# Local attention: blocks of 58 queries on two strips of 64 rows become blocks of 26 queries on four strips of 32, and VectorE turns the probabilities

## The chip, the core and the metric

One core of a Trainium2 chip runs one launch of the program. Its engines work side by side and wait for each other by semaphores: TensorE (PE in the profile, its weight loads PEld), VectorE (DVE), ScalarE (ACT), GpSimd (POOL), and SyncE (SP), which issues most transfers. Matmuls write to PSUM (eight banks here, tiles named `ps`); the other tiles lie in SBUF. The metric is the device time of one execution in microseconds.

## The reference, cut to what matters

Attention over 8 batches, 8 heads, 576 positions and a head size of 64 has two branches whose outputs are added. One averages q, k and v over groups of four and attends fully over 144 positions. The other, which the change rewrites, attends locally: a query sees the keys less than four positions away.

```
pos = np.arange(S)
mask = np.abs(pos[:, None] - pos[None, :]) < factor        # factor 4
scores = scale * np.matmul(q, k.transpose(0, 1, 3, 2))
scores = np.where(mask, scores, -1e9)
scores = scores - np.max(scores, axis=-1, keepdims=True)
attn = np.exp(scores)
attn = attn / (np.sum(attn, axis=-1, keepdims=True) + 1e-09)
out_local = np.matmul(attn, v)
```

The sum of the branches is the input x (8 x 576 x 512) of an MLP with a gate over positions: h = gelu(x w_in) is halved into u and v, v is normalized over its features and multiplied by a 576 x 576 matrix along the positions, and x + (u * v_s) w_out is the result.

## The kernel before

The work is cut into 32 attention pairs (a batch and two heads, which share the 128 partitions) and eight MLP passes, one a batch. Every step is a small task with a name: a letter or two and the pair's number (`S12`), or batch and part (`u3.4`). One table, `ORDER`, lists the more than 2,200 tasks in the order in which they are emitted, with a letter for the engine where there is a choice (V, A, P). Each engine runs its instructions in that order; `place` gives the buffers out by the same table. The MLP's matmuls keep fp32 accuracy by splitting both factors in a high and a low part and taking three products (lines 665 and 743).

A pair's tasks, local branch first:

- `S` (`scores`, L420): windows of 64 queries by 64 keys, ten a head, which advance by 58. The head's 64 features are the contraction. A window and a head write 64 rows of PSUM, so the ten windows of a head fill two strips of 64 rows in two banks. For the first four pairs (`EARLY_S`) an identity matmul puts the additive mask in PSUM first (L413).
- `ma`, `mb` (L428): VectorE adds the mask for the later pairs, PSUM to SBUF. `mx` takes the maxima, `nx` scales them to biases, `ea` and `eb` (L482) run ten exponentials on ScalarE, one for each column block, each with its own bias and its row sum. `re`, `rc`, `np` normalize (L504).
- `T` and a part of `U` (L512, L522): TensorE transposes the five 128x128 blocks of probabilities to PSUM; `pa` and `pb` copy them to SBUF.
- `D` (`av`, L573): values by probabilities, 64-row contractions, 20 matmuls on 64x64 parts of the array, and `xa`, `xb` (L580) add the other branch.

The averaged branch has `qs`, `ks`, `vs` (sums of four), `Y` (L442, scores), `my`, `ny`, `ec`, `nq`, its own transposes in `U` and `t` (L517), the copies `pc` and `pe`, `d` (`av_d`, L552: 72-row contractions) and `od`. Then `xh`, `xl`, `xc` split x for the MLP. Every non-transposing fp32 matmul of attention leaves two records in the trace. In the table the attention blocks stand between groups of MLP matmuls, mostly one or a few at a time.

Of the kernel before, what the change touches and what calls it, by code (L numbers as in the profile page):

```python
# [21 lines left out]
QB = 58  # L22
KB = 64
NT = 10
NTP = NT // 2
QPAD = QB * (NT - 1) + KB
HALF = S // 2
NS = 5
LEFT = S - 4 * P
XW = S + LEFT  # L30
# [54 lines left out]
lk0/S lq0/A ks0/V wy7 small wy2 lk1/A wuy7 qs0/V wby7 wqy7 wy0 lq1/S Y0 wy5 wy3 lq2 lk2 my0 wz7 wy1 wy4 wuy2 wz1 lq3  # L85
wz5 wy6 lk3 S0 wz2 lq4 wz0 wfy7 wby2 ny0/A wty7/P ks1/P wz4 wr1 lw3 lk4 wr2 lv0/S ec0 wqy2 wuy0 wby0 wqy0 why7/A
wuy5 mx0 wq2 lw2 lw0/S S1 wz6 lv1/S lk5 wr4 nx0/A qs1/P wfy0 lq5 wr7 wr0 lw1/S wq0 wfy2 wuy3 wby3 wby5 ea0 wqy3 eb0
wqy5 mx1 wuz7 re0/A wuy4 wty0/P wfy3 qs2/P nx1/V ea1 Y1 my1 wfy5 wly7/V ny1/V rc0 wby4 ec1 eb1 wqy4 wuz5 ks2/P
wty3/P wty5/P why5/V why0/V why3/V S2 mx2 np0/P Y2 my2 nx2/V ny2/V T0 re1/V wly5/V wfy4 pa0/V rc1 nq0/P wty2/P U0
pb0/V ec2 t0 wby1 ea2 wuy1 wuy6 wqy1 pc0/A wly3/P wty4/P wby6 nq1/P S3 wbz4 wqy6 np1/P why2/A wfy1 pe0/V qs3/P ks4/P  # L90
t1 mx3 wfy6 ks3/V eb2 wqz4 re2/A T1 wty6/P nx3/A wur2 pa1/A ea3 why4/A rc2 U1 qs4/V pb1/V pc1/A wuz2 d0 od0 lv2 wz3
np2/V why6/V wbz5 pe1/V wfz4 wqz5 T2 wty1/P nq2/P pa2/A wuz4 wly6/P wly4/P wly2/P wly0/P Y3 why1/V D0 wfz5 my3 xa0
U2 pb2/V xb0 pc2/V S4 wuz0 eb3 wur1 ny3/A ma4 xh0/V t2 pe2/A ec3 d1 mb4 wuz1 re3/A wuz6 wbz7 mx4 rc3 wbz6 Y4 od1 my4
D1 wbz0 qs5/P wtz5/P xl0/P np3/P nq3/P xc0 nx4/A wqz7 xa1 ea4 wqz6 ny4/A eb4 wq3 lv3 lw5 lw4 wq1 lk6 d2 wfz7 od2
wfz6 xb1 b lq6 wr3 wly1/V S5 lq7 lv4 ma5 xh1/V mb5 wtz7/P whz7/V mx5 wtz6/P t3 xl1/P ec4 re4/A whz5/A wqz0 rc4 vk2.0
D2 T3 nx5/A vk1.0 nq4/P xa2 pa3/A U3 wfz0 vk2.1 xb2 pb3/V eb5 np4/V vk1.1 xh2/V pc3/A wtz0/P ea5 wlz7/P wbz1 t4
pe3/V U4 vk0.0 wtz4/P xl2/P T4 pa4/A wqz1 pb4/A whq3/A ks6/V ks5/V qs6/V wfz1 d3 pc4/A od3 wur0 pe4/A wbz2 wbz3 wqz2
whz0/A wqz3 wuz3 vk1.2 D3 vs4 wr6 wr5 xa3 xb3 xh3/A wtz1/P whz1/A vk0.1 wlz0/P Y5 wfz2 d4 my5 od4 xl3/P wbr1 ny5/A
wur3 wqr1 wq4 lk7 wfz3 wur4 ec5 wlz1/V wur7 re5/A whz6/A wbr3 wqr3 wfr1 qs7/V wbr5 xc2 xc1 wtz3/P wlz5/P xc3 wtz2/P
wtr1/P rc5 np5/P wlz6/P vk2.2 vk0.2 v0.2 v0.1 v0.0 D4 wfr3 vg0.0 whz2/A whr1/A vg0.2 wqr5 whz3/A xa4 ks7/V vb0.0 xb4  # L100
v0.3 vg0.3 vp0.0 S6 vb0.2 ma6 wfr5 vn0.0 lk8 Y7 vg0.1 whq4/A wur5 whq1/A whz4/A vb0.1 wlz2/V mb6 my7 wlz3/P v0.4
u0.6 u0.4 u0.5 va0.4/A wbr7 vj0.4 xh4/A whq0/A whq2/A lq8 vp0.2 vp0.1 wtr5/P wtr3/P vg0.4 ny7/A u0.7 whr5/A wur6
whr3/A nq5/V vb0.3 vn0.1 wlz4/V vn0.2 wlq1/V wlq4/P vp0.3 u0.0 wlq2/P ua0.6 vh0.1/A ua0.4 ua0.5 u0.1 u0.2 vh0.0/A
ua0.7 vh0.2/A vb0.4 wqr7 ua0.0 vn0.3 vh0.3/A wbr2 wlr5/V wlq0/V wlr3/P vp0.4 vn0.4 wlq3/V vl0.0/V vl0.3/V vl0.2/V
wqr2 xl4/V vl0.1/P vh0.4/A u0.3 ua0.1 ua0.2 ua0.3 vl0.4/P wfr7 wfr2 Y6 mx6 my6 T5 s0.0 wlr1/P xc4 wtr7/P ks8/P qs8/P
sa0.0 wtr2/P sm0.0/P lv5 s0.1 U5 s0.2 ec7 wbr0 s0.3 pa5/A nx6/A whr7/A ea6 wbr4 sa0.1 wbr6 pb5/A wqr0 eb6 wqr6 wfr0
# [12 lines left out]
ea10 vh1.4/V vl1.4/V eb10 S11 os0.1 ma11 mb11 xb9 vl1.3/P vs10 lk13 lw11 os0.0 u1.5 lq13 re10/V rc10 s1.0 s1.4 mx11
ua1.6 ua1.5 np10/P T10 nq10/P U10 nx11/V ua1.7 xh9/A sa1.0 my11 eb11 ks13/P s1.2 ny11/V pa10/V pb10/V pc10/V t10  # L120
pe10/V sm1.0/P ks12/P xl9/P ea11 ec11 re11/A s1.1 sa1.2 sm1.2/V rc11 d10 sa1.1 s1.3 od10 lv11 np11/V sa1.4 sm1.4/V
sm1.1/V sa1.3 T11 nq11/P xc9 s1.5 U11 s1.6 t11 gh1.0/V sm1.3/V vs11 pa11/A s1.7 gh1.1/A pb11/A gl1.0/V sa1.5 sm1.5/V
pc11/A sa1.6 pe11/A gh1.2/A gl1.1/P D10 d11 od11 sm1.6/V sa1.7 sm1.7/V xa10 xb10 gl1.2/P S12 gh1.3/A D11 qs13/P lq14
ma12 Y12 gl1.3/V S13 xa11 mb12 ma13 mb13 my12 xb11 lk14 o1.7 Y13 xh11/A mx13 my13 nx13/V eb13 xh10/A o1.3 o1.0 o1.4
lk15 lq15 lw12 mx12 oa1.0 xl11/P xl10/P ks14/P xc10 lw13 o1.6 lv12 oa1.4 ny12/V xc11 vs12 nx12/A ny13/V ec13 ea12
ec12 qs15/V eb12 o1.1 v2.0 re12/A rc12 np12/P v2.1 ea13 oa1.1 nq12/P re13/V rc13 ks15/P qs14/V v2.2 T12 o1.5 vg2.1
t12 vg2.2 vg2.0 os1.0 oa1.6 vb2.1 oa1.7 np13/V os1.3 oa1.5 os1.2 u2.6 U12 pa12/V pb12/V vp2.1 vb2.2 vp2.2 vb2.0
vn2.1 o1.2 T13 u2.2 ua2.6 vp2.0 pc12/V vn2.0 pe12/V vh2.0/A vn2.2 nq13/V oa1.2 v2.4 va2.4/A vj2.4 vg2.4 vb2.4 pa13/V
ua2.2 u2.0 d12 od12 v2.3 ua2.0 D12 vp2.4 vl2.0/P lv13 vh2.2/V oa1.3 vn2.4 xa12 xb12 vg2.3 vh2.4/V vh2.1/A vs13 Y15
Y14 S14 U13 ma14 mb14 mx14 lq16 os1.1 u2.1 vl2.4/P vb2.3 pb13/A pc13/A xh12/V nx14/A t13 u2.3 u2.5 pe13/V ua2.1 my14  # L130
# [64 lines left out]
oa7.5 os7.2 oa7.7 os7.3.1  # L195
"""
EARLY_S, EARLY_D = 4, 4
SIZES = {"ps": 8, "X": 10, "R": 40}
WIDTH = {"ps": 512, "X": XW, "R": QPAD}


# [758 lines left out]
```

## Time and profile before

| | |
|---|---|
| time, median of 2 runs | 603.26 us (602.92 to 603.61) |
| the profiled execution's own time | 602.69 us |
| its span, first to last instruction | 600.9 us |
| busy: TensorE, VectorE, ScalarE, GpSimd | 578.5, 435.2, 336.2, 324.2 us |
| granted TensorE clock | 1.00 |
| moved by DMA | 58.08 MB |

The span is what the trace covers; 1.8 us of the execution lie around it. Matmuls overlap, so the length of one (0.2 to 0.4 us) is not what it costs; the distance between starts is. Rows of the timeline merge equal neighbours: start, time from the first start to the last end, line, shape, count.

### The profile page before, as it was taken

What the parts mean: (1) busy time and instruction counts of PE and PEld (TensorE: products, weight loads), DVE (VectorE), ACT (ScalarE), POOL (GpSimd) and SP (SyncE); (2) the same over time, 40 slices, a digit from 0 to 9 for tenths busy, and PEclk for the clock granted to TensorE, in tenths of its full rate; (3) what the DMA queues carried; (4) which work ended last, traced back from release to release, by engine and by line L of the source; (5) the groups of instructions that cost most, each with busy time, mean ns of one, the idle gap of its engine ahead of it and who ended that gap; (6) DMA issues with size and microseconds to landing.
All of it is one profiled execution on the core that took longest, in us unless ns stands there. A gap on an engine that the chain in (4) does not pass through costs nothing.

```text
span 600.9 us, 16628 instructions
## 1 busy us (share of the span) xinstructions
PE 578.5 (96%) x6544; PEld 524.9 (87%) x6544; DVE 435.2 (72%) x925; ACT 336.2 (56%) x1270; POOL 324.2 (54%) x417
## 2 busy tenths in 40 slices
PE   5599999999999999999999999999999999999997
PEld 3477889988999989988999889998999888998997
DVE  5999999758784798938786469774779478744652
ACT  5998875754936367264484537547473657811210
POOL 3788788644854255533365456534668554441221
DMA  8994103643040341404304123303225310201102
GB/s 311 349 313 147 42 21 97 192 122 100 25 124 23 100 144 44 124 0 140 106 25 140 62 83 113 112 22 102 61 83 168 96 28 1 80 5 39 40 1 79
DMA packets 28493, 58.08 MB, mean 97 GB/s; under 512 B 3328, under 2 KB 3584, under 8 KB 28416
## 3 DMA queue, kind: packets, MB, share of 16 engines
q1 hardware_dynamic: 28128, 56.43, 29.6%
q8 instruction: 51, 0.84, 0.6%
q10 hardware_dynamic: 288, 0.60, 0.3%
q14 instruction: 26, 0.21, 0.1%
HBM read 47.58 MB, written 9.44 MB: 95 GB/s over the span
## 4 chain that ended last, share of the span: by engine, by line
PE 79%; DVE 10%; DMA 4%; ACT 4%; issue 1%; POOL 1%; SPq 0%; DVEq 0%; ACTq 0%; POOLq 0%
PE ps L743 49%; PE ps L665 15%; PE ps L552 3%; PE ps L573 3%; PE ps L517 3%; PE ps L420 2%; DMA R<-in_w_in_dram 2%; PE ps L512 2%; PE ps L442 2%; ACT X L482 1%; DMA R<-in_qT_dram 1%; DVE R L222 1%; DMA X<-in_vw_dram 1%; DVE R L787 1%; DVE st L695 1%
## 5 line engine op out<-in xcount | busy, mean ns | idle before, releaser
L743 PE MATMUL ps<-wsg_h,R 128*128 128x288 f32 x576 | 122.8, 300 | 0.7 <-POOL R L734 0.7
L743 PE MATMUL ps<-R,wout_h 128*128 128x288 f32 x512 | 111.2, 302 | 0.4 <-DVE X L428 0.3
L482 ACT ACTIVATE X<-X,nb 128x64 f32<-128x64 f32 x280 | 93.5, 338 | 13.0 <-DVE nb L461 12.6
L743 PEld LDWEIGHTS ps<-wsg_h,R 128*128 128x128 f32 x576 | 93.7, 189 | 1.7 <-POOL R L734 0.9
L743 PE MATMUL ps<-wsg_l,R 128*128 128x288 f32 x320 | 92.6, 295 | 0.0
L743 PEld LDWEIGHTS ps<-R,wout_h 128*128 128x128 f32 x512 | 84.1, 188 | 3.6 <-issue 1.2
L743 PE MATMUL ps<-X,win_h 128*128 128x288 f32 x256 | 78.5, 307 | 1.0 <-DVE R L580 1.0
L743 PE MATMUL ps<-X,win_l 128*128 128x288 f32 x256 | 75.6, 295 | 0.0
L743 PE MATMUL ps<-R,win_h 128*128 128x288 f32 x256 | 75.6, 295 | 0.0
L743 PE MATMUL ps<-R,wout_l 128*128 128x288 f32 x256 | 75.6, 295 | 0.0
L706 POOL TENSOR_TENSOR rs<-rs,nhalf 128x1 f32<-128x1 f32 (+1 forms) x40 | 24.2, 606 | 85.9 <-DVE rs L697 85.8
L665 PE MATMUL ps<-win_h,X 128*128 128x512 f32 x160 | 65.4, 409 | 0.0
L665 PE MATMUL ps<-win_l,X 128*128 128x512 f32 x160 | 63.0, 394 | 0.0
L743 PEld LDWEIGHTS ps<-wsg_l,R 128*128 128x128 f32 x320 | 60.2, 188 | 0.0
L222 ACT COPY R<-ps 72x288 f32<-72x288 f32 (+2 forms) x87 | 32.7, 408 | 42.3 <-PE ps L517 14.9
L482 ACT ACTIVATION_READ_ACCUMULATOR X<-X,nb 128x1 f32 x280 | 53.4, 191 | 0.0
L743 PEld LDWEIGHTS ps<-X,win_h 128*128 128x128 f32 x256 | 48.2, 188 | 3.6 <-issue 1.6
L665 PE MATMUL ps<-win_h,R 128*128 128x512 f32 x128 | 50.5, 395 | 0.0
L222 ACT CAST R<-R 128x576 fp32r<-128x576 f32 (+2 forms) x35 | 22.6, 646 | 49.0 <-DVE R L714 21.0
L780 DVE SCALAR_TENSOR_TENSOR vs<-ps,small_sb,b_sb 128x288 f32<-128x288 f32 x64 | 32.3, 508 | 23.4 <-PE ps L743 21.7
L743 PEld LDWEIGHTS ps<-R,win_h 128*128 128x128 f32 x256 | 48.3, 189 | 0.3
L743 PEld LDWEIGHTS ps<-R,wout_l 128*128 128x128 f32 x256 | 48.2, 188 | 0.0
(102 smaller groups left out, 1417.1 us busy)
## 6 DMA issues: line engine op xcount, KB each, us to landing
X<-in_vw_dram SPq DMA_DIRECT2D x32, 320.0 KB
R<-in_v_dram SPq DMA_DIRECT2D x64, 144.0 KB
R<-in_kT_dram SPq DMA_DIRECT2D x31, 293.0 KB
R<-in_qT_dram SPq DMA_DIRECT2D x31, 293.0 KB
out_dram<-R SPq DMA_DIRECT2D x31, 288.0 KB
R<-in_w_in_dram SPq DMA_DIRECT2D x16, 256.0 KB
R<-in_w_out_dram SPq DMA_DIRECT2D x8, 256.0 KB
R<-in_w_sgT_dram SPq DMA_DIRECT2D x5, 288.0 KB
```

The lines of the kernel that those rows point to most:

```text
L222: (nc.scalar.copy if e == "A" else ENG[e].tensor_copy)(**kw)
L420: nc.tensor.matmul(out=sp[i][os, c * KB:(c + 1) * KB], lhsT=q[hs, t * QB:t * QB + KB], rhs=k[hs, t * QB:t * QB + KB], start=not early, sto ...
L442: nc.tensor.matmul(out=st["sdv"][n][os], lhsT=qd2[par][hs, i * 48:i * 48 + HD], rhs=st["kd"][hs], start=True, stop=True)
L482: nc.scalar.activation(out=st["ms"][:, t, :], in_=src, func=AF.Exp, bias=st["nb"][:, i * NTP + c:i * NTP + c + 1], scale=scale, accum_out= ...
L512: nc.tensor.transpose(out=t1[:, c * P:(c + 1) * P], in_=st["ms"][:, 2 * c:2 * c + 2, :], identity=ident_sb)
L517: nc.tensor.matmul(out=out[:, i * P:(i + 1) * P], lhsT=st["pd"][:, n, keys], rhs=ident2[:, i % 2], is_transpose=True, start=True, stop=True)
L552: nc.tensor.matmul(out=dn[hs].rearrange("p (i m) -> p i m", i=3), lhsT=st["v4"][kt][:, f, hs] if early_d else st["vd"][:, kt, hs], rhs=pdt ...
L573: nc.tensor.matmul(out=at["ps", "o", g, i][hs, c * QB:(c + 1) * QB], lhsT=v[ks, c, hs], rhs=pt[ks, c, h ^ i], start=True, stop=True)
L665: nc.tensor.matmul(out=acc, lhsT=r32(l), rhs=r32(w[:, k, DM:DF]), start=(i == 0 and ks[0] == 0), stop=(i == len(ops) - 1 and ks[-1] == KT ...
L706: nc.gpsimd.tensor_tensor(out=rs[0:n], in0=rs[0:n], in1=nhalf[0:n], op=ALU.pow)
L743: nc.tensor.matmul(out=acc[:, 0:HALF], lhsT=r32(l), rhs=r32(r), start=(first and n == 0), stop=(last and n == len(ops) - 1))
L780: nc.vector.scalar_tensor_tensor(out=vsb[i], in0=at["ps", "m", b, "s", i][:, 0:HALF], scalar=g_sb[:, i // 2:i // 2 + 1], in1=b_sb[:, half( ...
```

## The change

Local attention is cut into windows of 26 queries and 32 keys. The 23 windows of a head (24 places) lie on four strips of 32 rows, six column blocks each, so scores of a head fill one bank of 128 x 192. Rows of a window now hold one head only in each bank, and a block is 32 x 32, which VectorE can turn within SBUF. Part by part:

- `S`: 48 matmuls with a contraction of 64 and an output of 32 rows by 32 columns, with `tile_position` naming the part of the array; the mask matmuls have 192 columns instead of 320.
- Softmax: masked (`ma`, `mb`), maximum (`mx`), then the maximum is subtracted as an operation of its own (`sb`, on VectorE or GpSimd; for the first four pairs `ma` and `mb` do it straight from PSUM). One exponential covers all 384 columns, and the row sums are a VectorE reduce (`rw`). `nx`, `eb` and the accumulating forms are gone.
- `tr`: one VectorE transpose by 32x32 blocks takes the place of `T`, of the first matmul of `U`, and of `pa` and `pb`. `U` and `t` transpose 112 rows to 112 columns.
- `D`: 46 matmuls with a contraction of 32, outputs of 64 rows, up to 26 columns, into four banks, one for each strip; four merges (`x0` to `x3`) instead of two.
- SBUF pools are divided anew; the two halves of x lie in one tile `xx`. The value windows grow from 320 to 384 KB a pair. The order table is written anew throughout.

```
-QB = 58
-KB = 64
+QB = 26
+KB = 32
+NR = P // KB
+NC = 6
+NG = 2 * NC
...
-SIZES = {"ps": 8, "X": 10, "R": 40}
+SIZES = {"ps": 8, "X": 4, "M": 6, "H": 6, "R": 30}
...
+        def window(r, c):
+            return min((r * NC + c) * QB, S - QB)
+
         def scores(e):
             q, k = st["q"], st["k"]
...
+                for h in range(2):
+                    nc.tensor.matmul(out=sp[h][:, 0:NC * KB], lhsT=ident_sb, rhs=mask_sb, start=True, stop=False,
+                                     skip_group_check=True)
+            for c in range(NC):
+                for r in range(NR):
+                    w = slice(window(r, c), window(r, c) + KB)
                     for h in range(2):
...
+                        hs = slice(h * HD, (h + 1) * HD)
+                        nc.tensor.matmul(out=sp[h][r * KB:(r + 1) * KB, c * KB:(c + 1) * KB], lhsT=q[hs, w],
+                                         rhs=k[hs, w], start=not early, stop=True, skip_group_check=early,
+                                         tile_position=(h * HD, r * KB))
...
+        def below(e):
+            ENG[e].tensor_tensor(out=st["ms"], in0=st["ms"], in1=bc_last(stats[par][:, 0:NG], KB), op=ALU.subtract)
...
+        def exp(e):
+            nc.scalar.activation(out=st["ms"], in_=st["ms"], func=AF.Exp, scale=scale)
+
+        def row_sums(e):
+            nc.vector.tensor_reduce(out=sums[par][:, 0:NG], in_=st["ms"], axis=AX.X, op=ALU.add)
...
         def turn(e):
-            t1 = buf("ps", "t", g, 1)
-            for c in range(4):
-                nc.tensor.transpose(out=t1[:, c * P:(c + 1) * P], in_=st["ms"][:, 2 * c:2 * c + 2, :],
-                                    identity=ident_sb)
...
+            st["pt"] = buf("M", "pt", g)[:, 0:NG * KB].rearrange("p (t q) -> p t q", q=KB)
+            nc.vector.transpose(out=st["pt"].rearrange("p t q -> p (t q)"), in_=st["ms"].rearrange("p t k -> p (t k)"))
+
+        def turn_d(kt):
+            def emit(e):
+                out = buf("ps", "t", g, kt)
+                for i, n in ((0, 0), (1, 2), (2, 1)):
+                    nc.tensor.matmul(out=out[0:72, i * QD:(i + 1) * QD], lhsT=st["pd"][0:QD, n, kt * 72:(kt + 1) * 72],
+                                     rhs=ident2[0:QD, i % 2], is_transpose=True, start=True, stop=True)
+            return emit
...
         def av(e):
...
+            for c in range(NC):
+                for r in range(NR):
+                    t = r * NC + c
+                    if t < NT:
+                        q0 = t * QB - window(r, c)
+                        ks = slice(r * KB, (r + 1) * KB)
+                        for h in range(2):
+                            hs = slice(h * HD, (h + 1) * HD)
+                            nc.tensor.matmul(out=ob[r][hs, c * QB:c * QB + QB - q0], lhsT=v[ks, c, hs],
+                                             rhs=pt[ks, h * NC + c, q0:QB], start=True, stop=True,
+                                             tile_position=(r * KB, h * HD))
...
+        def merge(r):
+            def emit(e):
+                if r == 0:
+                    st["x"] = buf("R", "x", g)[:, 0:S]
+                c0 = r * NC * QB
+                n = min(NC * QB, S - c0)
                 nc.vector.tensor_tensor(
...
+                    out=st["x"][:, c0:c0 + n].rearrange("p (q f) -> p q f", f=2),
+                    in0=at["ps", "o", g, r][:, 0:n].rearrange("p (q f) -> p q f", f=2),
+                    in1=bc_last(od2[par][:, c0 // 2:(c0 + n) // 2], 2), op=ALU.add)
             return emit
...
-lk0/S lq0/A ks0/V wy7 small wy2 lk1/A wuy7 qs0/V wby7 wqy7 wy0 lq1/S Y0 wy5 wy3 lq2 lk2 my0 wz7 wy1 wy4 wuy2 wz1 lq3
+wy0 wby0 wqy0 wuy0 wy5 wy4 lk0/S wby5 wqy5 wuy4 wfy0 wuy5 wy3 wy2 wby4 wy7 wfy5 wy1 lq0/A wty0/P wqy4 wuy3 wby3 wfy4
```

On TensorE, in the steady part, a pair's transposes stood in one place before (L512 and L522 local, L517 averaged; L743 is the MLP):

```order
L743 MATMUL ps_2638<-wsg_l,R_2558 128x288
L512 MATMUL ps_2658<-small_sb,X_2428 128x128 x4
L522 MATMUL ps_2664<-small_sb,X_2428 128x128
L517 MATMUL ps_2664<-small_sb,R_2525 72x128 x3
L743 MATMUL ps_2684<-wsg_h,R_2258 128x288
```

At such a place there is now (L520 averaged, L739 the MLP):

```order
L739 MATMUL ps_3086<-wsg_h,R_2876 128x288
L739 MATMUL ps_3086<-wsg_l,R_2876 128x288
L520 MATMUL ps_3101<-small_sb,M_2999 72x112 x3
L739 MATMUL ps_3113<-wsg_h,R_2751 128x288
L739 MATMUL ps_3113<-wsg_h,R_2819 128x288
```

Only the averaged branch's three are left there, with 112 columns.

Where attention blocks stand side by side on TensorE, before, D (L573) ends, Y (L442) follows and S (L420) begins, all with 64-row, 64-column parts of the array:

```order
L573 MATMUL ps_2883<-R_2830,X_2603 64x58 x2
L573 MATMUL ps_2921<-R_2830,X_2603 64x58 x2
L442 MATMUL ps_2949<-kd_87,qd_79 64x144 x2
L442 MATMUL ps_2950<-kd_87,qd_79 64x144 x2
L442 MATMUL ps_2949<-kd_87,qd_79 64x144 x2
L420 MATMUL ps_2959<-R_2601,R_2619 64x64 x2
L420 MATMUL ps_2960<-R_2601,R_2619 64x64 x2
```

And now, with D at L564, Y at L447 and S at L424:

```order
L564 MATMUL ps_3436<-M_3280,X_2997 64x26 x2
L564 MATMUL ps_3437<-M_3280,X_2997 64x26 x2
L447 MATMUL ps_3490<-kd_87,qd_79 64x144 x2
L447 MATMUL ps_3491<-kd_87,qd_79 64x144 x2
L447 MATMUL ps_3490<-kd_87,qd_79 64x144 x2
L424 MATMUL ps_3498<-R_3080,R_3082 32x32
L424 MATMUL ps_3499<-R_3080,R_3082 32x32
L424 MATMUL ps_3498<-R_3080,R_3082 32x32
```

The blocks stand in the same sequence, but each of the three has a part of the array of its own shape: 32 rows by 64 columns, 64 by 64, 64 by 32.

On VectorE a pair's chain now reads as follows, with other tasks between (L435 mask, L458 maximum, L487 row sums, L503 reciprocal, L506 normalization, L514 turn; the subtraction of this pair is GpSimd's):

```order
L435 TENSOR_TENSOR M_4313<-ps_4258,small_sb 128x192
L435 TENSOR_TENSOR M_4313<-ps_4259,small_sb 128x192
L458 TENSOR_REDUCE stats_84<-M_4313 128x12
...
L487 TENSOR_REDUCE sums_86<-M_4313 128x12
L388 TENSOR_REDUCE kd_88<-R_4318 128x144
L783 TENSOR_TENSOR R_3861<-R_3861,vs_101 128x288
L503 RECIPROCAL rc_94<-sums_86 128x15
L795 TENSOR_TENSOR R_4474<-R_3997,R_4388 128x576
L506 TENSOR_TENSOR M_4313<-M_4313,rc_94 128x384
L514 STREAM_TRANSPOSE M_4477<-M_4313 128x384
```

Row sums and the turn are VectorE's new steps between the exponential and D.

More of the change, by code (lines that the diff above doesn't have):

```diff
@@ L90 @@
[L90 to L94, printed above, removed]
@@ L415, in scores @@
-            for c in range(NTP):
-                for i in range(2):
-                    t = 2 * c + i
-                    for h in range(2):
-                        hs, os = slice(h * HD, (h + 1) * HD), slice((h ^ i) * HD, ((h ^ i) + 1) * HD)
-                        nc.tensor.matmul(out=sp[i][os, c * KB:(c + 1) * KB], lhsT=q[hs, t * QB:t * QB + KB],
-                                         rhs=k[hs, t * QB:t * QB + KB], start=not early, stop=True,
-                                         skip_group_check=early)
```

462 lines of the change are left out of this document (210 added, 252 removed).

## The prediction

> **What bounds the kernel now.** The page comes first, for the shares, and then TensorE's waits and the busy time by stretch, for where its few idle microseconds lie.
>
> ```profile
> PE 578.5 (96%) x6544; PEld 524.9 (87%) x6544; DVE 435.2 (72%) x925; ACT 336.2 (56%) x1270; POOL 324.2 (54%) x417
> PE 79%; DVE 10%; DMA 4%; ACT 4%; issue 1%; POOL 1%; SPq 0%; DVEq 0%; ACTq 0%; POOLq 0%
> ```
> ```profile
> PE ps L442 <- DVE qd L387: 6.3, 1, 6.3
> PE ps L413 <- ACT R L490: 2.1, 1, 2.1
> PE ps L413 <- ACT X L482: 2.0, 1, 2.0
> ```
> ```profile
> 0.00:15.00 15.00, 7.84 (x112) 5.03 (x112) 7.84 (x20) 7.60 (x29) 5.71 (x16) 1.00 0.89 311
> 15.00:30.00 15.00, 8.84 (x136) 6.16 (x138) 14.52 (x40) 13.89 (x79) 11.99 (x17) 1.00 1.04 350
> 30.00:50.00 20.00, 17.75 (x355) 14.51 (x350) 19.82 (x47) 19.02 (x97) 16.57 (x21) 1.00 0.93 289
> 50.00:100.00 50.00, 48.29 (x471) 42.97 (x469) 47.32 (x103) 39.19 (x122) 40.67 (x49) 1.00 0.14 43
> 300.00:350.00 50.00, 50.00 (x539) 45.42 (x538) 33.35 (x68) 28.70 (x132) 27.32 (x37) 1.00 0.21 68
> ```
> In these stretches the first pair is TensorE's matmuls and weight loads, then VectorE, ScalarE, GpSimd. TensorE is idle for 15.6 us of the first 50 (7.2 + 6.2 + 2.2), while VectorE is nearly full and the DMA share is about 0.9 to 1.0. From 100 us on TensorE never waits for long; at 300 to 350 it is busy throughout and VectorE for 33 of 50. So a microsecond taken from TensorE's attention work after the start is a microsecond of the result, and one taken from ScalarE is worth nothing by itself.
>
> **The transposes.** A busy share says little of pipelined matmuls, so I read starts in the timeline: start, length, work, count.
>
> ```profile
> 161.26 0.29 PE L743 MATMUL ps<-wsg_l,R 128*128 128x288 f32 x1
> 161.40 0.60 PE L512 MATMUL ps<-small_sb,X 128*128 128x128 f32 x4
> 161.83 0.27 PE L522 MATMUL ps<-small_sb,X 128*128 128x128 f32 x1
> 161.94 0.49 PE L517 MATMUL ps<-small_sb,R 128*72 128x128 f32 x3
> ```
> Four transposes occupy 161.40 to 161.83, 0.108 us each. The five of a pair's local probabilities go (0.54 us); the six of the other branch keep their number and shrink from 128 to 112 columns (6 x 0.108 x 16/128 = 0.08). That is 0.62 us a pair, 19.8 us over 32 pairs. The copies out of PSUM that follow them go from ScalarE and VectorE.
>
> **Scores and values, S and D.** Each becomes more and smaller matmuls.
>
> ```profile
> 151.87 0.30 PE L743 MATMUL ps<-R,win_h 128*128 128x288 f32 x1
> 152.00 0.29 PE L743 MATMUL ps<-X,win_l 128*128 128x288 f32 x1
> 152.23 0.81 PE L573 MATMUL ps<-R,X 64*64 64x58 f32 x40
> 152.96 0.40 PE L743 MATMUL ps<-X,win_h 128*128 128x288 f32 x1
> 153.20 0.30 PE L743 MATMUL ps<-R,win_h 128*128 128x288 f32 x1
> ```
> ```profile
> L420 PE MATMUL ps<-R,R 64*64 64x64 f32 x1280 | 28.1, 225 | 0.7 <-DVE R L580 0.7
> L573 PE MATMUL ps<-R,X 64*64 64x58 f32 x1280 | 26.4, 222 | 0.2 <-ACT od L561 0.2
> L743 PEld LDWEIGHTS ps<-wsg_h,R 128*128 128x128 f32 x576 | 93.7, 189 | 1.7 <-POOL R L734 0.9 <-issue 0.6 <-ACT R L761 0.2
> L420 PEld LDWEIGHTS ps<-R,R 64*64 64x64 f32 x1280 | 24.1, 137 | 5.7 <-issue 2.6 <-DMA R<-in_w_in_dram 1.3 <-DVE R L580 1.2
> ```
> The code issues 20 matmuls for S and 20 for D; each leaves two records, which I call passes. Forty passes spread over four quarters of the array make ten rounds, and their last start is 0.81 - 0.22 = 0.59 us after the first: 0.059 us a round. S with 64 moving columns and D with 58 have the same length, so the moving columns don't set it. The load of 128 columns takes 189 ns and that of 64 takes 137, 0.81 ns a column; a 64-column load is worth 52 ns, near the whole round. I therefore take the weight load, with some 7 ns between passes, as what paces a round.
>
> Now S has 48 matmuls on eight tiles of 64x32, 12 passes on each tile, with 32 weight columns: by that pace 26 + 7 = 33 ns, 12 x 0.033 = 0.40 us, against 0.59. If a pass doesn't shrink it is 12 x 0.059 = 0.70. I take 0.40, since the two load rows are the nearest that show a width at work. D has 46 matmuls on eight tiles of 32x64, again 12 passes, but 64 weight columns each: 0.70. Both end on a shorter last pass (32 columns fewer, about 0.03 by the load's slope). So S changes by -0.22 us (bound +0.08), D by +0.08: -7.0 and +2.6 us over 32 pairs. Sixteen mask matmuls of the first four pairs shrink from 320 to 192 columns; at about 0.8 ns a column 16 x 128 columns are 1.7 us.
>
> The Trainium skill speaks against such tiles (TensorEngine Tiling (Array Packing), Instruction Overhead: about 60 cycles a matmul, and no tiling factor should come from a dimension that is already small). By that rule S would stay at its present pass and take the bound of 0.70; the load rows, which do scale, are why I don't take it.
>
> **Neighbours.** The tile shape also decides what a block costs beside another.
>
> ```profile
> 175.91 0.81 PE L573 MATMUL ps<-R,X 64*64 64x58 f32 x40
> 176.65 0.71 PE L552 MATMUL ps<-R,vd 72*64 72x144 f32 x8
> 177.29 0.81 PE L420 MATMUL ps<-R,R 64*64 64x64 f32 x40
> 177.92 0.76 PE L573 MATMUL ps<-R,X 64*64 64x58 f32 x40
> 178.50 0.31 PE L442 MATMUL ps<-kd,qd 64*64 64x144 f32 x4
> ```
> D followed by the 72-row d hands over after 0.74 us; D followed by the like-shaped Y after 0.58, and that block's own first pass is up to 0.05 shorter. A change of shape thus lets the array run empty, for 0.15 to 0.20 us. A block alone between MLP matmuls costs more still: from 152.00 to 153.20 is 1.20, less two MLP steps of 0.13 (151.87 to 152.00) it is 0.93 or 0.94, some 0.34 above its ten rounds. Standing beside a like shape saves that 0.34, beside an unlike one some 0.15.
>
> Before, S, Y and D all used 64x64 and overlapped. Afterwards they have 64x32, 64x64 and 32x64. Counting the order table, neighbours of like shape go from 43 to 2 and of unlike shape from 10 to 51. Saved before: 43 x 0.34 + 10 x 0.15 = 16.1 us; after: 2 x 0.34 + 51 x 0.15 = 8.3. This costs 7.8 us if 64x32 beside 64x64 empties the array as 72 rows beside 64 do. If it doesn't, 37 of the 51 overlap and 37 x 0.19 = 7.0 us come back. I take the emptying, as the row at hand shows it.
>
> The Trainium skill has it as a rule (TensorEngine Tiling (Array Packing), Key Properties: another tiling mode drains the array, another tile of the same mode does not). By that rule, the trace agrees for d; for two shapes of 32 no run here shows it.
>
> **The other engines.** ScalarE, VectorE and GpSimd rows that change:
>
> ```profile
> L482 ACT ACTIVATE X<-X,nb 128x64 f32<-128x64 f32 x280 | 93.5, 338 | 13.0 <-DVE nb L461 12.6
> L482 ACT ACTIVATION_READ_ACCUMULATOR X<-X,nb 128x1 f32 x280 | 53.4, 191 | 0.0
> L428 DVE TENSOR_TENSOR X<-ps,small_sb 128x320 f32<-128x320 f32 x56 | 26.0, 482 | 3.6 <-PE ps L420 3.2
> L453 DVE TENSOR_REDUCE stats<-X 128x10 f32<-128x640 f32 x28 | 22.7, 811 | 0.4
> L580 DVE TENSOR_TENSOR R<-ps,od 128x290 f32<-128x290 f32 x64 | 27.7, 448 | 19.8 <-PE ps L573 19.7
> L222 DVE CAST win_h<-R 128x256 fp32r<-128x256 f32 x6 | 4.4, 759 | 0.0
> L504 POOL TENSOR_TENSOR X<-X,rc 128x640 f32<-128x640 f32 x18 | 24.6, 1364 | 23.1 <-DVE rc L501 23.0 <-DMA R<-in_v_dram 0.2
> ```
> A pair's ten exponentials with their read-outs (10 x 0.53 us) become one of 384 columns, and ScalarE drops by over 4 us a pair; nothing waits for it in the steady part. VectorE: two mask adds go from 0.48 to 0.35 us (1.03 ns an element, from 482 ns for 320 and 811 for 640), the maximum from 0.81 to 0.54, the two merges of 0.45 become four of 0.26 to 0.31; new are row sums of 0.54 and the 32x32 turn, which no row shows (0.54 like a reduce of 384; up to 1.36, what GpSimd takes for 640). Gone from it are bias scalings and its share of copies. The sum is 0 to +0.6 us a pair, at most 20 us on an engine with 166 to spare; its cover is the 33-of-50 share above. At the start there is no cover, but five weight casts of 0.76 us move to ScalarE there. Where GpSimd has them, a subtraction and a normalization of 384 columns, 0.82 us each (1.36 x 384/640), replace one of 1.36.
>
> I allow 3.5 us (0 to 5) for TensorE time saved before 50 us, where it waits anyhow, and 1 us (0 to 6) for new waits. DMAs: the value windows grow by a fifth, queued two to four pairs ahead; nothing.
>
> **The sum.** -19.8 - 7.0 + 2.6 - 1.7 + 7.8 + 3.5 + 1.0 = -13.6 us. The profiled execution has a span of 600.9 inside 602.69 us, 0.57 under the median of 603.26; I apply the sum to the median: 589.7, said as 590. What a measurement of this kernel tells from no change is about 2%, 12.1 us: faster means under 591.2, slower over 615.3.
>
> **Rivals.**
> - Small matmuls don't shrink: S at 0.70 us, 9.6 us more, 599. For it: S and D are equal at 64 and 58 columns. Against: the load rows.
> - The new shapes overlap as like shapes did: 7.0 us less, 583. For it: all stay on quarter and eighth tiles of one array; against: the handover to d.
> - The longer vector chain makes TensorE wait. Masking, maximum, subtraction, exponential, sums, reciprocal, normalization and turn now all precede D, with three VectorE steps where matmuls and ScalarE stood, and GpSimd carries more of the start. About 10 us more, 600; against it VectorE's idle third and ScalarE's shorter part.
> - Slower: TensorE's sequencer paces small matmuls. Eighty loads and matmuls in 0.59 us are 7.4 ns an instruction; if that is issue and not weight load, S with 192 takes 1.42 us and D with 184 takes 1.36. S and D then add 32 x (2.78 - 1.24) = 49.4 us to the other terms (-9.2 us): 643. It decides from 4.1 ns an instruction on, where 376 x 4.1 ns eats the -9.2 us. For it: the equal lengths again. Against: they follow as well from equal 64-column loads.
>
> **Chances.** The forecast's case 0.45, small matmuls 0.33, overlapping shapes 0.08, vector chain 0.07, sequencer 0.07. The forecast's case spreads over 587 to 593, two thirds of it under 591.2. Faster: 0.30 + 0.08 = 0.38; slower 0.07 and a little for worse chains, 0.09; the same 0.53. The range of 582 to 603 leaves out the sequencer, the slower end of the chains and the lowest startup bound.
>
> **What will show it.** In the new trace: no 128x128 transposes of probabilities; S's first to last start at 0.4 or 0.7 us, D's at 0.7; handovers of S, Y and D at about 0.12 us after a last start or overlapped; PE's idle in 0 to 50 us still some 15 us, and waits on the turn or the subtraction small. The prediction is wrong if S or D runs past 0.8 us, or if TensorE waits after 100 us.

## The result, and the profile after

The changed kernel takes 644.5 us (median of 2 runs, 644.04 to 644.97) against 603.26: the ratio is 1.068, with a 95% interval of 1.064 to 1.073. It is slower by 41 us, where 590 was forecast; neither the range nor the sign held. The profiled execution has a span of 643.2 us.

The page of the kernel after, by the lines that were read before: engines with their busy time, share and instructions; the granted clock of TensorE in 40 slices; the queue that brings instructions; the chain by engine.

```profile
PE 595.4 (93%) x9840; PEld 537.6 (84%) x9840; DVE 428.1 (67%) x996; ACT 251.8 (39%) x643; POOL 321.5 (50%) x434
PEclk9987999799995999979999999989989999999999
q8 instruction: 77, 1.26, 0.8%
PE 87%; issue 5%; DMA 3%; DVE 3%; POOL 1%; ACT 0%; SPq 0%; POOLq 0%; DVEq 0%
```

The page of before has this line for the same queue:

```profile
q8 instruction: 51, 0.84, 0.6%
```

TensorE still bounds the kernel, and ScalarE has lost 84 us. But TensorE has half as many instructions again, "issue" is 5% of the chain instead of 1%, and the clock falls in places. The queue's numbers fit TensorE's program: 9,840 matmuls and 9,840 weight loads over 77 packets are 256 each, and 13,088 over 51 before are 257; 1.26 MB over 77 packets are 16 KB, so an instruction is 64 bytes.

TensorE's waits in the kernel after: what was waited for, us in all, times, the longest. Those put down to "issue" have no semaphore behind them; before, their largest line was 0.5 us.

```profile
PE ps L424 <- issue: 18.2, 10, 4.2
PE ps L417 <- DMA small_sb<-in_small_dram: 11.4, 1, 11.4
PE ps L564 <- issue: 5.2, 3, 2.3
PE ps L447 <- issue: 2.9, 2, 1.7
PE ps L539 <- issue: 2.1, 2, 1.4
```

They sum to 28.4 us. Busy time by stretch, in the same columns as before (TensorE's matmuls and loads, VectorE, ScalarE, GpSimd, clock, DMA share, GB/s):

```profile
0.00:15.00 15.00, 3.61 (x112) 2.99 (x112) 9.70 (x26) 7.89 (x19) 8.39 (x18) 1.00 0.89 301
15.00:30.00 15.00, 10.72 (x366) 8.20 (x362) 14.86 (x47) 13.84 (x52) 14.45 (x23) 1.00 1.03 350
30.00:50.00 20.00, 13.57 (x506) 11.05 (x507) 16.24 (x46) 14.08 (x45) 14.87 (x21) 0.90 0.95 278
100.00:150.00 50.00, 44.53 (x913) 39.20 (x912) 32.84 (x74) 14.72 (x39) 26.89 (x37) 0.93 0.29 87
...
190.00:194.60 4.60, 4.60 (x171) 4.10 (x169) 3.75 (x9) 1.57 (x4) 1.91 (x2) 1.00 0.48 144
194.70:196.60 1.90, 0.00 (x0) 0.00 (x0) 0.00 (x0) 0.48 (x1) 1.34 (x1) 0.85 0.90 265
196.70:210.00 13.30, 11.52 (x278) 10.18 (x279) 7.58 (x20) 4.21 (x13) 5.36 (x9) 0.51 0.08 26
...
300.00:350.00 50.00, 50.00 (x837) 45.61 (x835) 36.10 (x87) 18.39 (x52) 23.67 (x32) 1.00 0.31 98
```

The kernel before had this between 100 and 150 us:

```profile
100.00:150.00 50.00, 49.92 (x644) 43.98 (x642) 37.94 (x80) 28.28 (x114) 28.37 (x41) 1.00 0.49 151
```

From 100 us on, where TensorE had no idle time to speak of, 5.5 us are now missing by 150, and at 194.7 it stands still for 1.9 us while VectorE does nothing and ScalarE little, then goes on at a granted clock of 0.51 for 13 us. At 300 to 350 it is full as before. Its blocks in the timeline of the kernel after (start, first start to last end, work, count, and in brackets the idle time before):

```profile
193.34 0.71 PE L539 MATMUL ps<-R,vd 72*64 72x144 f32 x8
193.98 0.66 PE L424 MATMUL ps<-R,R 64*32 64x32 f32 x52
196.77 0.73 PE L424 MATMUL ps<-R,R 64*32 64x32 f32 x44 [2.14 <-issue]
...
301.17 0.30 PE L739 MATMUL ps<-H,win_l 128*128 128x288 f32 x1
301.31 0.45 PE L520 MATMUL ps<-small_sb,M 112*72 112x112 f32 x3
301.53 0.38 PE L739 MATMUL ps<-R,wout_h 128*128 128x288 f32 x1
...
317.94 1.12 PE L564 MATMUL ps<-M,X 32*64 32x26 f32 x92
318.99 0.71 PE L539 MATMUL ps<-R,vd 72*64 72x144 f32 x8
319.63 1.02 PE L424 MATMUL ps<-R,R 64*32 64x32 f32 x96
320.59 0.53 PE L739 MATMUL ps<-H,win_h 128*128 128x288 f32 x2
...
322.14 0.29 PE L739 MATMUL ps<-H,win_l 128*128 128x288 f32 x1
322.36 1.12 PE L564 MATMUL ps<-M,X 32*64 32x26 f32 x92
323.41 0.54 PE L739 MATMUL ps<-H,win_h 128*128 128x288 f32 x2
323.79 0.29 PE L739 MATMUL ps<-H,win_l 128*128 128x288 f32 x1
```

The five local transposes are gone, and the averaged ones, three at a place, are narrower. S (L424) runs 1.02 us and D (L564) 1.12; taking 0.20 us for a last pass, their last starts come 0.83 and 0.91 us after the first, against 0.59 before. A D alone among MLP matmuls costs 323.79 - 322.14 less three steps of 0.13, 1.25 us instead of 0.94. The first rows are the wait of the stretches above: a block of S stops after 52 of its 96 passes, though it waits for no semaphore, and stands for more than 2 us.

Where the 42 us of span went, by matmul starts in both traces (the time from one start to the next goes to the line of the first; of a distance over 0.9 us it keeps 0.3, and the rest is a line of its own), after less before:

| | us |
|---|---|
| transposes, local and averaged | -18.4 |
| mask matmuls | -2.4 |
| S | +10.1 |
| D | +13.2 |
| Y and d, the averaged branch | +8.5 |
| MLP matmuls (same number) | +6.1 |
| distances over 0.9 us, above 0.3 | +19.9 |
| first matmul later (6.3 to 11.4 us) | +5.1 |

The MLP's part is the clock: in the stretches that the clock's record has at half clock, 65 steps from one MLP matmul to the next take 0.24 us (their median) instead of 0.13, some 7 us more in all.

### The profile page after: what moved, and what is told of

It is laid out like the page before. It is cut to its first block, busy times and chain, and to the rows that moved or that the text cites. A ratio compares the mean times of both kernels' runs of the same rounds, so it can differ in the third digit from the quotient of the medians.

```text
span 643.2 us, 22661 instructions
## 1 busy us (share of the span) xinstructions
PE 595.4 (93%) x9840; PEld 537.6 (84%) x9840; DVE 428.1 (67%) x996; ACT 251.8 (39%) x643; POOL 321.5 (50%) x434
## 3 DMA queue, kind: packets, MB, share of 16 engines
q1 hardware_dynamic: 28272, 58.59, 28.4%
q8 instruction: 77, 1.26, 0.8%
## 4 chain that ended last, share of the span: by engine, by line
PE 87%; issue 5%; DMA 3%; DVE 3%; POOL 1%; ACT 0%; SPq 0%; POOLq 0%; DVEq 0%
PE ps L739 51%; PE ps L661 16%; PE ps L564 5%; PE ps L424 4%; PE ps L539 4%; PE ps L447 3%; PE ps L520 3%; DMA R<-in_v_dram 1%; DMA R<-in_w_in_dram 1%; DMA R<-in_kT_dram 1%; DVE R L730 0%; SPq L288 0%; DVE R L710 0%; POOL half L391 0%; DVE st L691 0%
## 5 line engine op out<-in xcount | busy, mean ns | idle before, releaser
L739 PE MATMUL ps<-wsg_h,R 128*128 128x288 f32 x576 | 122.0, 299 | 1.3 <-DVE R L730 1.3
L739 PE MATMUL ps<-R,wout_h 128*128 128x288 f32 x512 | 116.6, 313 | 0.2 <-DVE R L574 0.2
L739 PE MATMUL ps<-H,win_h 128*128 128x288 f32 x512 | 106.5, 302 | 0.0
L661 PE MATMUL ps<-win_h,H 128*128 128x512 f32 x288 | 99.8, 403 | 0.0
L739 PEld LDWEIGHTS ps<-wsg_h,R 128*128 128x128 f32 x576 | 93.8, 188 | 2.8 <-DVE R L730 1.5
L739 PE MATMUL ps<-wsg_l,R 128*128 128x288 f32 x320 | 92.5, 295 | 0.0
L739 PEld LDWEIGHTS ps<-R,wout_h 128*128 128x128 f32 x512 | 89.0, 199 | 2.9 <-issue 1.6
L739 PEld LDWEIGHTS ps<-H,win_h 128*128 128x128 f32 x512 | 83.1, 191 | 2.6 <-issue 1.2
L739 PE MATMUL ps<-R,wout_l 128*128 128x288 f32 x256 | 78.3, 306 | 0.0
L739 PE MATMUL ps<-H,win_l 128*128 128x288 f32 x256 | 76.1, 297 | 0.0
L661 PEld LDWEIGHTS ps<-win_h,H 128*128 128x128 f32 x288 | 54.2, 188 | 13.5 <-issue 1.2
L661 PE MATMUL ps<-win_l,H 128*128 128x512 f32 x160 | 63.3, 396 | 0.0
L739 PEld LDWEIGHTS ps<-wsg_l,R 128*128 128x128 f32 x320 | 60.2, 188 | 0.0
L424 PE MATMUL ps<-R,R 64*32 64x32 f32 x3072 | 35.6, 206 | 18.9 <-issue 18.2
L424 PEld LDWEIGHTS ps<-R,R 64*32 64x32 f32 x3072 | 30.6, 110 | 26.4 <-issue 22.6
L574 DVE TENSOR_TENSOR R<-ps,od 128x156 f32<-128x156 f32 (+1 forms) x128 | 34.2, 296 | 27.2 <-PE ps L564 24.3
L739 PEld LDWEIGHTS ps<-R,wout_l 128*128 128x128 f32 x256 | 51.1, 200 | 0.0
L739 PEld LDWEIGHTS ps<-H,win_l 128*128 128x128 f32 x256 | 48.9, 191 | 0.0
```

The lines of the kernel that those rows point to most:

```text
L424: nc.tensor.matmul(out=sp[h][r * KB:(r + 1) * KB, c * KB:(c + 1) * KB], lhsT=q[hs, w], rhs=k[hs, w], start=not early, stop=True, skip_grou ...
L574: nc.vector.tensor_tensor(out=st["x"][:, c0:c0 + n].rearrange("p (q f) -> p q f", f=2), in0=at["ps", "o", g, r][:, 0:n].rearrange("p (q f) ...
L661: nc.tensor.matmul(out=acc, lhsT=r32(l), rhs=r32(w[:, k, DM:DF]), start=(i == 0 and ks[0] == 0), stop=(i == len(ops) - 1 and ks[-1] == KT ...
L739: nc.tensor.matmul(out=acc[:, 0:HALF], lhsT=r32(l), rhs=r32(r), start=(first and n == 0), stop=(last and n == len(ops) - 1))
```

## The experiments

Two theories from the traces. **Supply**: instructions don't reach the array fast enough. Within a block they pace the passes; where blocks stand in a row, TensorE runs out of them, waits for the next packet, and then works at half clock. The count of loads and matmuls decides. **Shape**: tiles of 64x32 and 32x64 are slow in the array itself, and the waits belong to the change of shape; fewer or more instructions change little.

### Fewer matmuls, the same shapes

S with 24 matmuls of 64 keys instead of 48 of 32. Every second block's scores are then wrong.

```
-            for c in range(NC):
+            for c in range(0, NC, 2):
...
+                    w2 = slice(min(window(r, c), QPAD - 2 * KB), min(window(r, c), QPAD - 2 * KB) + 2 * KB)
...
-                        nc.tensor.matmul(out=sp[h][r * KB:(r + 1) * KB, c * KB:(c + 1) * KB], lhsT=q[hs, w],
-                                         rhs=k[hs, w], start=not early, stop=True, skip_group_check=early,
+                        nc.tensor.matmul(out=sp[h][r * KB:(r + 1) * KB, c * KB:(c + 2) * KB], lhsT=q[hs, w],
+                                         rhs=k[hs, w2], start=not early, stop=True, skip_group_check=early,
```

> The changed kernel with 24 matmuls a pair for S instead of 48: each covers two column blocks (64 keys) with the query window of the first, so every second block has wrong scores. Supply theory (TensorE starts the first 64 queued instructions of a block quickly, then one per about 4.2 ns, and the instruction stream, fetched in pieces of 16 KB, runs dry in bursts): S falls from 0.83 us first to last start to about 0.35, the 28 us of waits without a releaser fall to about 10, the clock rises, and the time is about 608 us. Shape theory (32-column parts of the array are slow in themselves, whatever the number of matmuls): S stays at 0.8 us or grows with the wider matmuls, waits stay, 640 to 650 us.

D with 24 matmuls of up to 52 columns instead of 46, with every second block's probabilities met by the wrong values:

```
-                    if t < NT:
+                    two = 2 if t + 1 < NT and t * QB == window(r, c) and (t + 1) * QB == window(r, c + 1) else 1
+                    if t < NT and (c % 2 == 0 or t == NT - 1):
...
-                            nc.tensor.matmul(out=ob[r][hs, c * QB:c * QB + QB - q0], lhsT=v[ks, c, hs],
-                                             rhs=pt[ks, h * NC + c, q0:QB], start=True, stop=True,
+                            nc.tensor.matmul(out=ob[r][hs, c * QB:c * QB + two * QB - q0], lhsT=v[ks, c, hs],
+                                             rhs=pt[ks, h * NC + c:h * NC + c + two, q0:QB], start=True, stop=True,
```

> The changed kernel with 24 matmuls a pair for D instead of 46: each takes the probabilities of two column blocks with the values of the first, so every second block's output is wrong. Supply theory: D falls from 0.91 us first to last start to about 0.37, waits without a releaser fall to about 10 us, about 606 us. Shape theory: D stays at 0.9 us or more, 640 to 650 us.

And both together:

> Both of these at once: S and D with 24 matmuls each, the same tile shapes and the same order of tasks. Supply theory: waits without a releaser nearly gone, granted clock back at 1.0, 644 - 32 (blocks) - 27 (waits) - 6 (clock), about 580 us. Shape theory: still 640 us or more.

Measured, with the first-to-last start of S and D and the waits put down to issue:

| kernel | loads and matmuls | S, D us | issue waits us | time us | ratio to before |
|---|---|---|---|---|---|
| after | 19,680 | 0.83, 0.91 | 28.4 | 644.5 | 1.068 |
| S wide | 16,608 | 0.51, 0.91 | 4.4 | 609.4 | 1.011 (1.009 to 1.013) |
| D wide | 16,864 | 0.83, 0.53 | 17.2 | 623.4 | 1.034 (1.032 to 1.036) |
| both wide | 13,792 | 0.51, 0.53 | 0 | 594.2 | 0.984 (0.982 to 0.986) |

The waits of TensorE with both wide have no issue line left; the longest are:

```profile
PE ps L417 <- DVE ps L299: 11.0, 1, 11.0
PE ps L566 <- DMA X<-in_vw_dram: 2.9, 1, 2.9
PE ps L540 <- ACT M L485: 2.6, 1, 2.6
PE ps L741 <- DVE R L732: 1.3, 1, 1.3
```

The same columns through parts of the array of the same shapes, with half the loads and passes in S and D (30% fewer instructions in all), take 50 us off. All of it lies behind the two hundredth MLP matmul, which comes at 98.0 us with both wide and at 98.8 after, although 9.1 of the 28.4 us of waits stood ahead of it. Behind it, by starts as in the table above, S gives 10.3 us, D 11.5, the distances over 0.9 us 17.9, and the MLP's matmuls 7.6, because the 34 us at half clock that the kernel after has there are gone: 47.3 of 49.6 us. With S alone wide it is 10.4, 0.4, 13.9 and 7.1 of 34.3; with D alone 1.7, 11.3, 2.5 and 1.2 of 19.0, since other waits, for VectorE and GpSimd, came in place of some that went. Shape is out as the main cause. The expected sizes were less good than the direction: S and D came down to 0.51 and 0.53 us, not to 0.35 and 0.37. The time is 17 us above the expected one for D alone, which is about the waits that stayed, and 14 above for both: S and D gave 21.8 us there instead of 32, and the waits at the start that went brought nothing.

### The block's own pace

The same 48 matmuls of S, from the fifth pair on with 64 moving columns instead of 32 wherever the next block exists:

```
+                    two = 2 if not early and c < NC - 1 and window(r, c) + 2 * KB <= QPAD else 1
+                    w2 = slice(window(r, c), window(r, c) + two * KB)
...
-                        nc.tensor.matmul(out=sp[h][r * KB:(r + 1) * KB, c * KB:(c + 1) * KB], lhsT=q[hs, w],
-                                         rhs=k[hs, w], start=not early, stop=True, skip_group_check=early,
+                        nc.tensor.matmul(out=sp[h][r * KB:(r + 1) * KB, c * KB:(c + two) * KB], lhsT=q[hs, w],
+                                         rhs=k[hs, w2], start=not early, stop=True, skip_group_check=early,
```

> The changed kernel with the same 48 matmuls for S, but each streams 64 keys instead of 32 where the next column block follows, and the next matmul overwrites the second half with the right scores (pairs 0 to 3 as they are). The number of instructions is the same, the work of the array nearly doubles. If instructions pace S (some 8.3 ns for a load and a matmul), S stays at 0.83 to 0.87 us and the time within 4 us of 644. If the array paces it, 32 more columns at 0.83 ns are 27 ns more a round, S becomes 1.1 us or more, and the time 650 or more.

645.8 us (641.5 and 650.2, too far apart to say more of the time); S rises from 0.83 to 0.93 us, past what the one theory expected (0.87) and short of the other (1.1). In its timeline:

```profile
324.10 1.12 PE L426 MATMUL ps<-R,R 64*32 64x64 f32 x96
```

Twice the columns cost 0.10 us a block, so the columns are not the main thing that sets it, but a little shows. The single starts (a median over 22 undisturbed S blocks of the kernel after and 29 of D; ns from the first start, by the number of the pass) say when it begins:

```
pass       0    8   16   24   28   36   44   60   76   88  last
S after    0   52   92  125  145  313  380  513  647  747   830
D after    0   79  138  196  223  360  443  579  751  861   911
```

The first 32 passes, 64 loads and matmuls, start within 0.17 us (S) and 0.24 us (D). From the 36th on, S goes at (747 - 313)/52 = 8.3 ns a pass, 4.2 ns a load or matmul, and D, with twice the weight columns, at (861 - 360)/52 = 9.6. The last passes are slower still (747 to 830 for seven of S), for a reason that no run shows. The kernel before had only 40 passes in a block. Within the first 24 passes a round of eight takes 33 to 52 ns in S and 58 to 79 in D, near the 33 and 59 ns that the prediction worked with: the array can go at that pace, and what holds it back comes later in the block.

### The old shape, twice as many instructions

The kernel before, with S and D issued twice, both from the fifth pair on:

```
-            for c in range(NTP):
+            for c in [c for c in range(NTP) for _ in range(1 if early else 2)]:
```

> The kernel before, with every matmul of S (from pair 4 on) and of D issued twice: 160 instructions a block on 64x64 parts of the array, no new shapes. Blocks grow by ten rounds of 0.059 us in either theory: 603 + 28 x 0.59 + 32 x 0.59 = 638 us. Supply theory: bursts now outrun the instruction fetch here too, waits without a releaser appear, some 5 to 15 us with the clock's loss: 643 to 653 us. Shape theory: none appear, 636 to 640 us.

656.1 us, ratio 1.088. S and D run 1.18 us, twice 0.59. TensorE's waits in this kernel:

```profile
PE ps L420 <- issue: 9.8, 7, 3.8
PE ps L573 <- issue: 3.9, 2, 2.0
PE ps L552 <- issue: 3.0, 1, 3.0
```

The edit doubles D too for 28 pairs only, where the expectation counted 32: it should have said 636, not 638. The 56 more blocks' worth of passes at 0.59 us are 33.0 us and make 636.1 from the 603.1 of the kernel before beside it. The other 20.0 are these 16.7 us of waits and 3.3 us by which the MLP's matmuls are longer by their starts, with 20 us at half clock. That is more than either theory had expected (643 to 653 at most), but the waits need no new shape: 17,568 instructions on 64x64 call them forth too. Within a block the old shape keeps its 59 ns a round to the end, 7.4 ns an instruction, slower than the 4.2 above. This fits the weight load as the pace there, as the prediction had it. It doesn't prove it: in the run with 64 moving and 32 weight columns S also takes 56 ns for each round of eight from its 8th to its 24th pass.

### Fewer blocks in a row

The kernel after, with only the order table altered: behind the start, MLP matmuls are put between an S or a D and its neighbour where dependences allow it. One of the places:

```
-u0.6 lv6 nq6/P sm0.5/P gh0.1/V sa0.7 sm0.4/V gh0.2/A ks8/P gl0.0/P s0.6 gl0.1/V gl0.2/V ua0.6 D5 S7 lw7
+D5 u0.6 lv6 nq6/P sm0.5/P gh0.1/V sa0.7 sm0.4/V gh0.2/A ks8/P gl0.0/P s0.6 gl0.1/V gl0.2/V ua0.6 S7 lw7
```

> The changed kernel with the same instructions; only the order table is altered, so that behind the first stage two MLP blocks stand between any two of S and D where that was possible. Supply theory: the waits without a releaser behind 100 us go from some 18 us to under 4 and those of the start stay; the clock rises to 0.99; some 20 more blocks stand alone at 0.2 us: about 626 us. Shape theory: every block costs what it did, and more stand alone: 644 to 650 us.

641.6 us (638.5 to 643.0), ratio 1.063: 3 us gained where 18 were expected. The waits it has:

```profile
PE ps L422 <- issue: 2.2, 2, 1.4
PE ps L659 <- DVE R L809: 2.1, 1, 2.1
PE ps L562 <- issue: 1.9, 1, 1.9
PE ps L537 <- ACT R L222: 1.7, 3, 0.6
PE ps L737 <- DVE R L572: 1.6, 1, 1.6
PE ps L562 <- DVE M L512: 1.4, 1, 1.4
```

With a third line of 0.4 us, the waits for instructions fell from 28.4 to 4.5 us, and behind 60 us none is left: bursts of blocks cause them. But it was given back. By starts, the distances over 0.9 us give 17.3 us and S 2.4, while Y and d take 4.8 us more, the MLP 4.3, D 3.9, and transposes and masks 3.2. TensorE now waits more for VectorE and ScalarE, there are 112 groups of blocks between MLP work instead of 103, and by the clock's record the half clock in the first 60 us grew from 10 to 34 us. How much each of these three took was not measured apart.

### The start

TensorE's first matmul of the MLP comes at 55.2 us instead of 43.2, its two hundredth at 98.8 instead of 90.4. Here the loads of the mask, of `lk0` and `lq0` were put first and the second pair's value loads (`lv1`, `lw1`) earlier:

```
-wy0 wby0 wqy0 wuy0 wy5 wy4 lk0/S wby5 wqy5 wuy4 wfy0 wuy5 wy3 wy2 wby4 wy7 wfy5 wy1 lq0/A wty0/P wqy4 wuy3 wby3 wfy4
-wby2 ks0/P wty5/P small why0/A wqy3 wz5 wfy3 wuy7 wuy2 why5/A wqy2 wuy1 wly0/P wby7 wqy7 wz4 lk1/S wfy2 wby1 wqy1
...
+small lk0/S lq0/A wy0 wby0 wqy0 wuy0 wy5 wy4 wby5 wqy5 wuy4 wfy0 wuy5 wy3 wy2 wby4 wy7 wfy5 wy1 wty0/P wqy4 wuy3 wby3
+wfy4 wby2 ks0/P wty5/P why0/A wqy3 wz5 wfy3 wuy7 wuy2 why5/A wqy2 wuy1 wly0/P wby7 wqy7 wz4 lk1/S wfy2 wby1 wqy1 lq1/S
```

> The changed kernel with five loads earlier in the order table: the mask tile and the first pair's q and k first of all, and the second pair's value tiles ahead of the second half of w_out. If the first stage is late because TensorE's first blocks wait for these loads, its first matmul starts at 4 to 6 us instead of 11.4, the first MLP matmul at about 50 instead of 55, and the time is about 639 us. If the start is paced by the weights' preparation and by instruction fetch, the time stays at 642 to 646 us.

651.6 us (649.7 to 653.0), and the MLP's first matmul comes later still, at 58.7, with 34 us at half clock around it. The first wait is not for the mask's transfer any more but for VectorE:

```profile
PE ps L415 <- DVE R L312: 9.7, 1, 9.7
```

Both expectations missed: the first matmul came at 9.7 us, not at 4 to 6, and the start got longer. Bringing these loads forward does not bring the start forward. With S and D wide the start is late as well (the two hundredth MLP matmul at 98.0), so it isn't the number of matmuls either. Which of the chains through VectorE, ScalarE and GpSimd holds it stays open.

### The transposes, put back and made narrow

The kernel after, with five transposes of 128 columns a pair issued again, of a constant, ahead of the averaged ones:

```
                 out = buf("ps", "t", g, kt)
+                for i in range(3 if kt == 0 else 2):
+                    nc.tensor.transpose(out=out[:, i * P:(i + 1) * P], in_=ident_sb, identity=ident_sb)
```

> The kernel after with five more 128x128 transposes a pair (of a constant, into the PSUM tiles that the averaged transposes then overwrite), three ahead of U's three and two ahead of t's: the same work on TensorE that the change took away, nothing else. Two theories of what its removal was worth. By the starts in the two traces a pair's transposes fell from 1.17 to 0.60 us, of which five of 128 columns at 0.109 us are 0.54; then putting them back costs 32 x 0.54 = 17.4 us, 662 us (659 to 666, the upper end with more waits for instructions). If transposes start in the shadow of their neighbours and the difference of starts is only shifted between lines, they cost half of that or less: under 654 us.

666.9 us (662.0 to 668.6): 22.4 us more than after, at the upper end of what was expected or just past it. By starts the 160 transposes take 19.7 us, 0.123 each, and 2.7 are left for the rest. What the change took away was worth what it was priced at.

The kernel before, with nothing but its averaged transposes cut from 128 to the 112 rows and columns in use (and a constant that they multiply with, to match):

```
-                nc.tensor.matmul(out=out[:, i * P:(i + 1) * P], lhsT=st["pd"][:, n, keys], rhs=ident2[:, i % 2],
+                nc.tensor.matmul(out=out[:, i * P:i * P + 112], lhsT=st["pd"][0:112, n, keys], rhs=ident2[0:112, i % 2, 0:112],
                                  is_transpose=True, start=True, stop=True)
```

> The kernel before with one part of the change alone: the averaged branch's transposes take 112 rows to 112 columns instead of 128 to 128. 192 transposes at 0.095 instead of 0.108 us are 2.6 us of TensorE's stream, about 2.3 of them behind the start: 600.6 us, a ratio of 0.996. If transposes of this kind cost by the instruction and not by the column, no change.

601.49 us (11 runs) against 603.09 (16 runs): ratio 0.9972, 0.9959 to 0.9986. This one part of the change, alone, is faster than the kernel before, by 0.3%.

## Why the prediction was wrong

- **The bound** was read rightly: TensorE before and after; the shorter ScalarE part (2.6 us a pair, where over 4 were reckoned) and the new VectorE steps show in none of TensorE's longer waits in the steady part.
- **Transposes**, -19.8: right. -18.4 by starts, and +19.7 when five were put back.
- **S and D**, -7.0 and +2.6: here the sum failed first. The step was "I therefore take the weight load, with some 7 ns between passes, as what paces a round". The old blocks fit it, also doubled, and so do the first 64 loads and matmuls of the new ones; but it was carried through blocks of 96 passes. What the runs show in its place is a second limit: past the first 64 instructions they come 4.2 ns apart or a little more (the table of starts). That it hangs on the count of instructions is shown by the wide kernels; what sets the 4.2 ns, no run shows. S took 0.83 us, not 0.40, and D 0.91, not 0.70; against 0.59 that is 32 x (0.24 + 0.32) = +17.9 us where -4.4 stood. The bound of +0.08 us for S was no bound, since it held the pass at its old length and asked only how many passes each tile had, never how many all tiles had together. The Trainium skill's warning (TensorEngine Tiling (Array Packing), Instruction Overhead), which was weighed and put aside, pointed the right way; as it is worded, by the length of a single matmul, it gave 0.70 for S, and the measured 0.83 lies beyond that.
- **New waits**, +1.0 (0 to 6): the second failure, and the larger. In the trace of before only one wait of 0.5 us spoke of it; 28.4 us of waits for instructions came, and behind them the half clock, which the sum did not have at all and which cost the MLP's matmuls alone some 7 us. The prediction did write that it would be wrong "if S or D runs past 0.8 us, or if TensorE waits after 100 us"; both came.
- **Neighbours**, +7.8: right, as far as it can be told apart. At every change of shape the next block starts late: D hands over to d 0.14 us after its last start (rows at 317.94 and 318.99), and by the starts (medians) D to Y after 0.14, S to Y after 0.12, Y to S after 0.21, where the like shapes of before took 0.04, 0.04 and 0.01. The Trainium skill's rule (TensorEngine Tiling (Array Packing), Key Properties) thus holds for these shapes too.
- **The start**, +3.5 (0 to 5): the two hundredth MLP matmul comes 8.4 us later, outside its bounds, cause open.
- **The sum without the failed terms.** The kernel with both wide tests it. From the two hundredth MLP matmul to the last it takes 491.4 us, where before took 507.1: -15.7. By starts this is -15.1 for transposes, -2.5 for S and D, +5.1 for Y and d, -1.6 for the MLP and -1.5 for distances over 0.9 us. The blocks' own lengths (25 of S and 27 of D, 0.08 and 0.06 us shorter) are -3.6, so that handovers and first passes took some 6 us of the 7.8 that were forecast for the whole kernel.
- **The rivals.** The sequencer rival gave 643 us (it took 1.24 us for S and D before; its own 0.59 for each are 1.18, which would make 645), and its point of decision, 4.1 ns an instruction, was passed: 0.83 + 0.91 us for 376 instructions are 4.6. But its size came right by accident. It took 7.4 ns from the old blocks, whose pace the new ones left behind, and put all of its 49 us into S and D; they took 18 more than before, and the rest came by waits and the start, of which it said nothing. It had 0.07; the equal lengths of S and D were read for it and against it, and a count over whole bursts, of which the prediction has none, might have raised it: D, d and S in a row, from 317.94 to 320.59, are now 392 instructions in 2.65 us.

The fetching can be followed in the records. The packets around the wait at 194 us begin at 194.25, 197.88, 201.82 and 205.57 us and take 0.9 to 1.25 us each. In this window the transfers by queue are:

```profile
q1 hardware_dynamic: 744, 1.49, 24.6%
q8 instruction: 4, 0.07, 1.3%
```

256 instructions come every 3.6 to 3.9 us here. Over the whole kernel one packet in 8.4 us would do (643.2/77), but a burst like D, d and S uses 256 up in 1.7. Now number TensorE's recorded instructions from zero, loads, matmuls and semaphore instructions together (19,848). All 16 waits put down to issue that last over 0.4 us end with an instruction whose number is 193 plus a whole multiple of 256, and it starts 1.2 to 1.7 us after a packet of this queue has landed. The same holds for 67 of the 69 such waits in the other runs; the two left over are a wait of 0.5 us near 19 us that the kernel before has too. So what ends these waits is the arrival of the next 256 instructions. Why a packet comes late, and where the 1.2 us behind its landing go, stays open; no run moved a packet.

## What to carry to other kernels

Count loads and matmuls, not only columns: in this kernel a matmul that is split into smaller tiles costs at least 8.3 ns for each pass with its load once a block has over 64 instructions, and a row of such blocks costs more, since the next 256 instructions may not be there. A limit that the old code stays under leaves hardly a trace in its profile (one wait of 0.5 us here), so a change that raises a count by half needs that count worked out against time for the densest stretch, not only the mean. And of a change with a good part and a bad one, try the parts alone: the narrower transposes were worth 0.3% by themselves, and the same tiling with half the matmuls would have been worth 1.6%, if blocks could be found for which it computes the right thing.

## What the hardware showed that was not expected

- The first 64 loads and matmuls of a block start within 0.17 to 0.24 us, 2.6 to 3.8 ns each; beyond that they start 4.2 ns apart on tiles with 32 weight columns and 4.8 with 64.
- A block can stop in its middle for up to 4.2 us with no semaphore in play: always ahead of the first of 256 instructions, which starts 1.2 to 1.7 us after their packet has landed.
- After most such waits the clock stays at half for 3.4 to 13.7 us: 0.51 was granted from 196.7 to 210. Of the nine behind 100 us, the three that end at 139.0, 388.3 and 439.7 us (1.2 to 1.4 us long) have none. In the whole kernel after it is 44 us by the clock's record, in the profiled execution of before none. Other waits do it too: with both wide, 27 of the first 62 us are at half clock without a wait for instructions. The Trainium skill (TensorE: Matmul & The Clock Gate, What's actually happening) gives an idle window of about 3.4 us for the fall; here the record falls at 196.0, when TensorE had stood still for some 1.4 us.
